# Dividing the attention numerators by their sum before the transposes, not after the weighted sum, from batch 1 on

## The chip, the cores and the metric

The kernel runs on one core of one Trainium2 chip. The metric is the time on the device in microseconds (us), the median of three runs. The core has five engines with a queue of their own each, and they meet only through semaphores: TensorE (PE in the profile, its weight loads PEld), VectorE (DVE), ScalarE (ACT), GpSimd (POOL) and SyncE (SP, which issues the DMAs). Every engine takes its queue in order.

## The reference, cut to what matters

The program is a top-32 attention over 8 batches, 8 heads, 576 positions and a head width of 64, and behind it a gated feed-forward network (FFN) over the 4608 tokens.

```python
scores = scale * np.matmul(q, k.transpose(0, 1, 3, 2))        # 8, 8, 576, 576
kth = np.partition(scores, -top_k, axis=-1)[..., -top_k:-top_k + 1]
scores = np.where(scores >= kth, scores, -1000000000.0)
scores = scores - np.max(scores, axis=-1, keepdims=True)
attn = np.exp(scores)
attn = attn / (np.sum(attn, axis=-1, keepdims=True) + 1e-09)
x = np.matmul(attn, v)                                        # tokens x 512, heads side by side
gate = 1.0 / (1.0 + np.exp(-(x @ w_gate)))
return gate * (x @ w_val) @ w_out
```

## The kernel before

**Steps.** Attention is cut into steps of one batch b, one row tile i and one pair of heads p. Tiles i = 0 to 3 hold 128 rows of two heads (J = 2 halves, called j = 0 and j = 1 below); tile i = 4 holds the last 64 rows of both heads in one half (J = 1). That makes 5 x 4 = 20 steps in a batch and 160 in all. A batch is walked in two groups of row tiles: 0 to 2 and 3 to 4 in an even batch, 0 to 1 and 2 to 4 in an odd one; within a group the four pairs follow each other.

**What a step does.** `scores` multiplies queries and keys on PE (L195) and ACT brings each half from PSUM into the tile `s` (L202). `select` finds the 32nd largest score of each row on DVE (L260 to L266, L286), helped by ACT (L272) and POOL (L278, L279), and ACT takes the exponentials into the tile `e` (L209). `masked` then sets what is below the threshold to zero and sums each row, in one DVE instruction for each half (L214); POOL adds 1e-9 to the sums in the small tile `st` (L217) and DVE takes the reciprocals (L218). POOL spreads the reciprocals over a 128 x 128 tile `inv` (L220), 64 columns for each head.

**Turning and weighing.** `turn` transposes `e` on PE in groups of three 128 x 128 blocks (L297, L302, L305); ACT copies each group from PSUM into `et` (L298, L303, L306). The first group needs half j = 0 alone, the second both halves, the third half j = 1. `weigh` multiplies `et` with the values on PE (L316 to L318 for full tiles, L321 to L324 for the last 64 rows), for one or two row tiles at once, into the left part `po` of one PSUM tile. Into the right part PE transposes `inv` of each of these row tiles (L327). ACT copies these spread reciprocals to SBUF as `rs` (L330), DVE multiplies `po` with them into `xf` (L333, L337), ACT rounds `xf` to the leading part `xh` (L340) and POOL subtracts to get the rest `xl` (L341). `xh` and `xl` are the FFN's input. `weigh` is called 112 times: 48 times with two row tiles (256 columns), 32 times with one (128 columns), and 32 times with the last 64 rows. So `inv` is turned 160 times.

**FFN.** Units of 384 tokens run as a generator beside the attention (`ffn`): 12 hidden blocks of 24 matmuls each (L372 to L374), gated by ACT, DVE and POOL (L377 to L380), and three rounds of output matmuls (L391 to L393). The loop in `run` takes pieces from the generators by the attention's progress, less a lag of 480 tokens (`BEHIND`). In the first 60 % of batch 0 the FFN's weights are split and stored too (`split_weight`, L116 to L148).

**What sets the order.** The program is written step by step with three stages in flight (`select` of step n, `masked` of step n-1, `turn` and `weigh` of step n-2), and the tile framework's scheduler then lays out each engine's queue from the dependences, its pools and its own estimates. Pools that matter here: `e` has three buffers, `et` two, the PSUM tile of `weigh` one, the PSUM of the scores one, of the transposes two, and of the FFN three. A second version of the whole program stands behind a test at the end (`run(True)`), for inputs on which the fast selection fails; it isn't executed here.

Of the kernel before, what the change touches and what calls it, by code (L numbers as in the profile page):

```python
# [15 lines left out]
AF = mybir.ActivationFunctionType  # L16
ALU = mybir.AluOpType
AX = mybir.AxisListType

TOPK = 32  # L20
# [8 lines left out]
def tile_topk_attention_then_gated_ffn(  # L29
# [8 lines left out]
    nc = tc.nc  # L38
# [3 lines left out]
    HALF = S // 2  # L42
# [19 lines left out]
    BEHIND = 480  # L62

    LOADED, HELD = 12, 0

    const = ctx.enter_context(tc.tile_pool(name="const", bufs=1))
    bi = ctx.enter_context(tc.tile_pool(name="bi", bufs=4))
# [25 lines left out]
    kths = const.tile([P, n_tiles + 8], F32, tag="kths", name="kths")  # L93
# [114 lines left out]
        for j in range(J):  # L208
            nc.scalar.activation(e[:, j], s[:, j], AF.Exp, bias=st[:, j : j + 1], scale=1.0 / SHRINK)  # L209

    def masked(J, s, kth, st, e, nm):

        for j in range(J):
            nc.vector.scalar_tensor_tensor(  # L214
                e[:, j], s[:, j], kth[j], e[:, j], op0=ALU.is_ge, op1=ALU.mult, accum_out=st[:, 4 + j : 5 + j]
            )
        nc.gpsimd.tensor_scalar(st[:, 4 : 4 + J], st[:, 4 : 4 + J], 1e-9, None, op0=ALU.add)  # L217
        nc.vector.reciprocal(st[:, 6 : 6 + J], st[:, 4 : 4 + J])  # L218
        inv = bi.tile([P, P], F32, tag="inv", name=f"inv_{nm}")
        nc.gpsimd.tensor_copy(  # L220
            inv.rearrange("p (j d) -> p j d", j=J), st[:, 6 : 6 + J].unsqueeze(2).to_broadcast([P, J, P // J])
        )
        return e, inv

    def select_any(J, s, nm):

        rest = b2.tile([P, 2, S + 8], F32, tag="u", name=f"rest_{nm}")[:, :, :S]
        tops = b2.tile([P, 2, TOPK], F32, tag="tops", name=f"tops_{nm}")
        st = bi.tile([P, 8], F32, tag="st", name=f"st_{nm}")
        e = b3.tile([P, 2, S], F32, tag="e", name=f"e_{nm}")  # L230
        for r in range(TOPK // 8):
            for j in range(J):
                t = tops[:, j, 8 * r : 8 * r + 8]
                src = rest[:, j] if r else s[:, j]
                nc.vector.max(t, src)
                if r < TOPK // 8 - 1:
                    nc.vector.match_replace(rest[:, j], t, src, LOWEST)
        nc.gpsimd.tensor_scalar(st[:, 0:J], tops[:, :J, 0], -1.0 / SHRINK, None, op0=ALU.mult)
        numerators(J, s, st, e)
        yield  # L240
        yield masked(J, s, [tops[:, j, TOPK - 1 :] for j in range(J)], st, e, nm)

    def select(J, s, col, nm):

# [37 lines left out]
        at = [n_tiles - col - j for j in range(J)]  # L284
        for j in range(J):
            nc.vector.max(kths[:, at[j] : at[j] + 8], u[:, j])  # L286
        yield masked(J, s, [kths[:, a + 7 : a + 8] for a in at], st, e, nm)

    def turn(e, i, et, o, nm):

# [17 lines left out]
    def weigh(et, vt, n, invs, pieces, nm):  # L308

        both = ps_o.tile([P, 4 * P], F32, tag="o", name=f"po_{nm}")  # L310
        po, rb = both[:, :n], both[:, 2 * P :]
        if n > REM:
            mixed = vt[:, 4:6].rearrange("p a d -> p (a d)")

            for c in reversed(range(4)):
                nc.tensor.matmul(po[D:], vt[:, 6 + c], et[:, 5 + c, :n], start=c == 3, stop=False)  # L316
                nc.tensor.matmul(po[:D], vt[:, c], et[:, c, :n], start=c == 3, stop=False)
            nc.tensor.matmul(po, mixed, et[:, 4, :n], start=False, stop=True)  # L318
        else:
            for c in range(4):  # L320
                nc.tensor.matmul(po[:D], vt[:, c], et[:, c, :REM], start=c == 0, stop=False)  # L321
                nc.tensor.matmul(po[D:], vt[:, 6 + c], et[:, c, REM:P], start=c == 0, stop=False)
            nc.tensor.matmul(po[:D], vt[:REM, 4], et[:REM, 4, :REM], start=False, stop=True)
            nc.tensor.matmul(po[D:], vt[:REM, 10], et[:REM, 4, REM:P], start=False, stop=True)  # L324

        for t, inv in enumerate(invs):
            nc.tensor.transpose(rb[:, t * P : (t + 1) * P], inv, ident)  # L327
        rs = b2.tile([P, 2 * P], F32, tag="rs", name=f"rs_{nm}")
        m = len(invs) * P
        nc.scalar.activation(rs[:, :m], rb[:, :m], AF.Copy)  # L330
        xf = b2.tile([P, 2 * P], F32, tag="xf", name=f"xf_{nm}")[:, :n]
        if n > REM:
            nc.vector.tensor_tensor(xf, po, rs[:, :n], op=ALU.mult)  # L333
        else:
            for h in range(2):
                d = slice(h * D, h * D + D)
                nc.vector.tensor_tensor(xf[d], po[d], rs[d, h * REM : h * REM + REM], op=ALU.mult)  # L337
        o = 0
        for (xh, xl), c, k in pieces:
            nc.scalar.activation(xh[:, c : c + k], xf[:, o : o + k], AF.Copy)  # L340
            nc.gpsimd.tensor_tensor(xl[:, c : c + k], xf[:, o : o + k], xh[:, c : c + k], op=ALU.subtract)  # L341
            o += k
# [61 lines left out]
    def run(general):  # L404
# [30 lines left out]
        parts, done = {}, {}  # L435

        for n in range(len(steps) + 2):
            if n < len(steps):
# [12 lines left out]
                J = 2 if i < NT else 1  # L451
                nm = f"{mark}{b}_{i}_{p}"
                if general:
                    parts[n] = select_any(J, staged.pop(n), nm)
                else:
                    parts[n] = select(J, staged.pop(n), col, nm)
                next(parts[n])
                col += J
            if n - 1 in parts:
# [113 lines left out]
```

## Time and profile before

| | before |
|---|---|
| median of 3 runs | 1626.93 us (1625.65 to 1627.8) |
| the profiled execution | 1628.2 us on the device, span 1626.3 us |
| PE busy | 1546.3 us, 95 % of the span |
| PE weight loads busy | 1399.8 us, 86 % |
| DVE busy | 1285.6 us, 79 % |
| POOL busy | 1238.9 us, 76 % |
| ACT busy | 1174.1 us, 72 % |
| mean granted TensorE clock | 0.977 of full speed |

The span runs from the first to the last instruction on the engines; the time on the device is 1.9 us more. Matmuls are pipelined: the profile gives each its whole passage through the array, so the durations of neighbours overlap, and the distance between their starts is shorter than the duration of one. Busy time is the union of what overlaps.

### The profile page before, as it was taken

The numbers are of one execution on the slowest core, as the hardware profiler recorded it, in microseconds if no ns is written. First come the engines' busy times: TensorE is split into PE (matmuls) and PEld (weight loads), VectorE is DVE, ScalarE is ACT, GpSimd is POOL, SyncE is SP. The second block draws the span as 40 slices with busy tenths as digits, with TensorE's granted clock in tenths as the row PEclk, the third lists the DMA queues.
The fourth block names the chain that finished last, engine by engine and source line by source line (L and its number), as shares of the span: only waits on it lengthen the run. The fifth ranks groups of instructions, "written<-read, shape, count | busy, mean of one in ns | idle before, by whom it ended". The sixth has DMA issues, their size and how long they took to land.

```text
span 1626.3 us, 33530 instructions
## 1 busy us (share of the span) xinstructions
PE 1546.3 (95%) x10226; PEld 1399.8 (86%) x10226; DVE 1285.6 (79%) x5748; ACT 1174.1 (72%) x2643; POOL 1238.9 (76%) x1959
## 2 busy tenths in 40 slices
PE   5777899899999999999999999999999999999998
PEld 3444797689999999989999999999899999999997
DVE  6999868988988778878888778889888778878310
ACT  8898668877777777677777777778677777767321
POOL 8889868898876887787776896788876987776413
PEclk8887999999999999999999999999999999999999
DMA  7546754566565665566564665565555665554574
GB/s 259 186 161 201 266 203 167 186 225 217 189 218 178 219 236 198 184 207 227 193 206 178 219 239 195 196 230 195 203 199 178 216 224 198 184 198 164 195 265 178
DMA packets 89182, 332.58 MB, mean 204 GB/s; under 512 B 9888, under 2 KB 36512, under 8 KB 62112
## 3 DMA queue, kind: packets, MB, share of 16 engines
q1 hardware_dynamic: 88992, 330.34, 58.7%
q8 instruction: 83, 1.36, 0.3%
q14 instruction: 107, 0.88, 0.2%
HBM read 301.99 MB, written 28.31 MB: 203 GB/s over the span
## 4 chain that ended last, share of the span: by engine, by line
PE 75%; DVE 5%; POOL 5%; ACT 4%; issue 1%; POOLq 0%; ACTq 0%; DVEq 0%
PE pz L372 11%; PE pz L374 11%; PE pz L373 11%; PE pss L195 8%; PE po L316 6%; PE pt L297 6%; PE po L391 6%; PE po L392 5%; PE po L393 5%; PE po L318 2%; POOL u L278 2%; DVE e L214 2%; ACT e L209 1%; PE po L327 1%; DVE kths L286 1%
## 5 line engine op out<-in xcount | busy, mean ns | idle before, releaser
L278 POOL TENSOR_TENSOR u<-s,under 128x288 f32<-128x288 f32 x576 | 446.1, 796 | 89.0 <-ACT under L272 82.7
L260 DVE MAX8 cand<-s 128x8 f32<-128x72 f32 x2304 | 346.7, 217 | 81.4 <-ACT s L202 80.7
L372 PE MATMUL pz<-xh,w 128*128 128x384 f32 x1120 | 383.3, 344 | 1.7 <-ACT part L398 1.7
L373 PE MATMUL pz<-xl,w 128*128 128x384 f32 x1120 | 379.5, 339 | 0.0
L374 PE MATMUL pz<-xh,w 128*128 128x384 f32 x1120 | 379.4, 339 | 0.0
L214 DVE SCALAR_TENSOR_TENSOR e<-s,kths,e 128x576 f32<-128x576 f32 x288 | 297.1, 1035 | 1.9 <-ACT e L209 1.8
L286 DVE MAX8 kths<-u 128x8 f32<-128x584 f32 x288 | 219.7, 763 | 71.0 <-POOL u L279 69.0
L272 ACT ACTIVATE under<-s,leads 128x576 bf16<-128x576 f32 x288 | 223.2, 776 | 42.2 <-DVE leads L264 38.0
L209 ACT ACTIVATE e<-s,st 128x576 f32<-128x576 f32 x288 | 210.7, 773 | 57.5 <-POOL st L268 57.4
L380 POOL TENSOR_TENSOR gl<-gf,gh 128x384 fp32r<-128x384 f32 x144 | 153.5, 1066 | 88.8 <-ACT gh L379 86.3
L202 ACT ACTIVATE s<-pss 128x576 f32<-128x576 f32 x288 | 185.3, 643 | 39.0 <-PE pss L195 38.9
L372 PEld LDWEIGHTS pz<-xh,w 128*128 128x128 f32 x1120 | 210.9, 188 | 2.5 <-ACT part L398 2.0
L195 PE MATMUL pss<-k,qh 128*128 128x288 f32 (+2 forms) x672 | 200.6, 316 | 13.1 <-ACT qh L176 6.6
L373 PEld LDWEIGHTS pz<-xl,w 128*128 128x128 f32 x1120 | 210.9, 188 | 0.4 <-issue 0.3
L374 PEld LDWEIGHTS pz<-xh,w 128*128 128x128 f32 x1120 | 210.7, 188 | 0.0
L298 ACT ACTIVATE et<-pt 128x384 f32<-128x384 f32 x384 | 180.8, 489 | 36.5 <-PE pt L297 35.6
L297 PE MATMUL pt<-ident,e 128*128 128x128 f32 x1152 | 188.0, 280 | 16.6 <-DVE e L214 14.9
L392 PE MATMUL po<-gl,w 128*128 128x384 f32 x560 | 192.2, 344 | 0.4 <-POOL gl L380 0.4
L391 PE MATMUL po<-gh,w 128*128 128x384 f32 x560 | 189.4, 352 | 1.8 <-ACT part L398 0.9
L393 PE MATMUL po<-gh,w 128*128 128x384 f32 x560 | 189.7, 340 | 0.0
L195 PE MATMUL pss<-k,ql 128*128 128x288 f32 (+2 forms) x672 | 185.1, 298 | 1.0 <-POOL ql L177 1.0
L297 PEld LDWEIGHTS pt<-ident,e 128*128 128x128 f32 x1152 | 145.4, 144 | 37.9 <-DVE e L214 16.2
(100 smaller groups left out, 3339.2 us busy)
## 6 DMA issues: line engine op xcount, KB each, us to landing
w<-ws SPq DMA_DIRECT2D x210, 1024.0 KB, 5.0
v<-in_v_dram SPq DMA_DIRECT2D x64, 352.0 KB, 3.4
qraw<-in_q_dram SPq DMA_DIRECT2D x160, 128.0 KB, 2.8
kraw<-in_k_dram SPq DMA_DIRECT2D x64, 288.0 KB, 3.4
wraw<-in_w_dram SPq DMA_DIRECT2D x36, 512.0 KB, 4.1
ws<-wsplit SPq DMA_DIRECT2D x36, 512.0 KB, 4.0
out_dram<-acc SPq DMA_DIRECT2D x48, 192.0 KB, 3.6
```

Source lines behind the costliest of these rows:

```text
L195: nc.tensor.matmul(ps[:, half, o : o + n], x[:, h * P : (h + 1) * P], ks[h][:, k0 : k0 + n], start=t == 0, stop=t == len(todo) - 1,)
L214: nc.vector.scalar_tensor_tensor(e[:, j], s[:, j], kth[j], e[:, j], op0=ALU.is_ge, op1=ALU.mult, accum_out=st[:, 4 + j : 5 + j])
L260: nc.vector.max(cand[:, j, 8 * g : 8 * g + 8], s[:, j, g * SEG : (g + 1) * SEG])
L278: nc.gpsimd.tensor_tensor(u[:, j, c], s[:, j, c], under[:, j, c], op=ALU.mult)
L286: nc.vector.max(kths[:, at[j] : at[j] + 8], u[:, j])
L297: nc.tensor.transpose(pt[:, c], ef[:, k0 : k0 + P], ident)
L372: nc.tensor.matmul(ps, wt[:, u, 0, d], xh, start=d == 0, stop=False)
L373: nc.tensor.matmul(ps, wt[:, u, 0, d], xl, start=False, stop=False)
L374: nc.tensor.matmul(ps, wt[:, u, 1, d], xh, start=False, stop=d == NP - 1)
L391: nc.tensor.matmul(ps, wt[:, e % 2, 0, f], gh, start=f == 0, stop=False)
L392: nc.tensor.matmul(ps, wt[:, e % 2, 0, f], gl, start=False, stop=False)
L393: nc.tensor.matmul(ps, wt[:, e % 2, 1, f], gh, start=False, stop=f == FG - 1)
```

## The change

From batch 1 on (`b < TURNED` with `TURNED = 1` keeps the old way for batch 0), the masked numerators `e` themselves are multiplied by the reciprocal of their row's sum, in place: half j = 0 in one instruction on ACT, half j = 1 (where there is one) in two instructions of 288 columns on POOL. No `inv` is made, none is transposed, and there are no `rs` and no `xf`: ACT rounds `po` straight from PSUM to `xh`, and DVE, which can read PSUM, subtracts to get `xl`.

```diff
-    def masked(J, s, kth, st, e, nm):
+    def masked(J, s, kth, st, e, turned, nm):
...
         nc.vector.reciprocal(st[:, 6 : 6 + J], st[:, 4 : 4 + J])
+        if not turned:
+            for j in range(J):
+                if j == 0:
+                    nc.scalar.activation(e[:, j], e[:, j], AF.Copy, scale=st[:, 6 + j : 7 + j])
+                    continue
+                for half in range(2):
+                    c = slice(half * HALF, (half + 1) * HALF)
+                    nc.gpsimd.tensor_scalar(e[:, j, c], e[:, j, c], st[:, 6 + j : 7 + j], None, op0=ALU.mult)
+            return e, None
         inv = bi.tile([P, P], F32, tag="inv", name=f"inv_{nm}")
...
+        o = 0
+        if invs[0] is None:
+            for (xh, xl), c, k in pieces:
+                nc.scalar.activation(xh[:, c : c + k], po[:, o : o + k], AF.Copy)
+                nc.vector.tensor_tensor(xl[:, c : c + k], po[:, o : o + k], xh[:, c : c + k], op=ALU.subtract)
+                o += k
+            return
         for t, inv in enumerate(invs):
             nc.tensor.transpose(rb[:, t * P : (t + 1) * P], inv, ident)
...
-                    parts[n] = select(J, staged.pop(n), col, nm)
+                    parts[n] = select(J, staged.pop(n), col, b < TURNED, nm)
```

The scheduler lays the queues out anew. Three places show how, all around batch 4, row tiles 0 to 2, pair 1. In the names the numbers behind a tile's name are batch, row tile and pair (then a buffer number); `gh`, `gl`, `po2`, `acc` and `w_5_...` belong to FFN unit 5. Line numbers are those of each kernel's own file.

PE's queue at the end of the weighing of row tiles 0 and 1, before:

```order
L317 MATMUL po_4_1_1_12522<-et_4_0_1_12349,v_8_1_11658 64x256
L318 MATMUL po_4_1_1_12522<-et_4_0_1_12349,v_8_1_11658 128x256
L327 MATMUL po_4_1_1_12522<-ident_102,inv_4_0_1_12138 128x128
L327 MATMUL po_4_1_1_12522<-ident_102,inv_4_1_1_12312 128x128
L297 MATMUL pt_4_2_1_1_12662<-ident_102,e_4_2_1_12267 128x128 x3
L297 MATMUL pt_4_2_1_2_12667<-ident_102,e_4_2_1_12267 128x128 x3
```

and in the changed kernel:

```order
L328 MATMUL po_4_1_1_12321<-et_4_0_1_12147,v_8_1_11468 64x256
L329 MATMUL po_4_1_1_12321<-et_4_0_1_12147,v_8_1_11468 128x256
L408 MATMUL po2_5_0_3_12567<-gh_5_0_0_11980,w_5_13_12549 128x384
L409 MATMUL po2_5_0_3_12567<-gl_5_0_0_11981,w_5_13_12549 128x384
L410 MATMUL po2_5_0_3_12567<-gh_5_0_0_11980,w_5_13_12549 128x384
```

The two transposes of `inv` are gone, and FFN matmuls follow the last product directly; the transposes of row tile 2, which stood behind them, come later.

POOL's queue around the reciprocals of row tile 1, before:

```order
L177 TENSOR_TENSOR ql_4_0_3_12247<-qraw_4_0_3_12244,qh_4_0_3_12246 128x256
L217 TENSOR_SCALAR st_4_1_1_12091<-st_4_1_1_12091 128x2
L220 COPY inv_4_1_1_12312<-st_4_1_1_12091 128x128
L268 TENSOR_SCALAR st_4_2_1_12265<-tops_4_2_1_12264 128x2
L380 TENSOR_TENSOR gl_5_0_1_12317<-gf_5_0_1_12344,gh_5_0_1_12316 128x384
```

and in the changed kernel:

```order
L397 TENSOR_TENSOR gl_5_0_2_12237<-gf_5_0_2_12264,gh_5_0_2_12236 128x384
L219 TENSOR_SCALAR st_4_1_1_11892<-st_4_1_1_11892 128x2
L228 TENSOR_SCALAR e_4_1_1_11894<-e_4_1_1_11894,st_4_1_1_11892 128x288 x2
L179 TENSOR_TENSOR ql_4_1_3_12166<-qraw_4_1_3_12163,qh_4_1_3_12165 128x256
L289 TENSOR_TENSOR u_4_2_1_12065<-s_4_2_1_11727,under_4_2_1_12066 128x288 x2
```

Where the copy to `inv` stood, directly behind the addition of 1e-9, the two multiplications of half j = 1 stand now; between the two on POOL lies the reciprocal on DVE, as before.

ACT's queue in the changed kernel, from the exponentials of row tile 2 to the first copy of the transposed row tile 1:

```order
L211 ACTIVATE e_4_2_1_12064<-s_4_2_1_11727,st_4_2_1_12062 128x576 x2
L394 ACTIVATE gf_5_0_3_12299<-pz_5_0_3_0_12273 128x384
L224 ACTIVATE e_4_1_1_11894<-e_4_1_1_11894,st_4_1_1_11892 128x576
L178 ACTIVATE qh_4_1_3_12165<-qraw_4_1_3_12163 128x256
L204 ACTIVATE s_4_0_2_11877<-pss_4_0_2_1_11884 128x576
L283 ACTIVATE under_4_2_1_12066,sums_4_2_1_12063<-s_4_2_1_11727,leads_119 128x576
L396 ACTIVATE gh_5_0_3_12271<-gf_5_0_3_12299 128x384
L283 ACTIVATE under_4_0_2_12188,sums_4_0_2_12185<-s_4_0_2_11877,leads_119 128x576
L309 ACTIVATE et_4_0_1_12147<-pt_4_1_1_0_12304 128x3x128
```

The division of half j = 0 (L224) is a new row in this queue. It stands six rows ahead of the copy of the first transposed blocks of the same tile, with an eviction of scores (L204), two rows of the selection (L283) and two of other work between.

## Rows read from the trace of the kernel before

**Rows 1.** Busy time of each engine in four stretches of the span, in us: while batch 0 ends, in the middle, while the attention runs out, and (the last row) from 200 to 1500 us as a whole. The columns are the stretch, its length, and the busy us (and instructions) of PE, PEld, DVE, ACT and POOL, then the granted clock, the DMAs' share and GB/s.

```profile
150.00:200.00 50.00, 39.79 (x258) 33.17 (x257) 45.16 (x166) 34.75 (x78) 46.83 (x71) 0.93 0.71 251
...
700.00:900.00 200.00, 200.00 (x1375) 186.86 (x1375) 169.70 (x777) 146.89 (x334) 154.08 (x250) 1.00 0.60 205
...
1500.00:1560.00 60.00, 60.00 (x398) 56.52 (x397) 18.75 (x60) 21.98 (x50) 24.75 (x35) 1.00 0.59 206
...
200.00:1500.00 1300.00, 1284.89 (x8804) 1188.97 (x8804) 1080.51 (x4948) 972.24 (x2217) 1021.28 (x1641) 1.00 0.59 203
```

**Rows 2.** The page's chain of work that ended last, as shares of the span by engine and by engine and line.

```profile
PE 75%; DVE 5%; POOL 5%; ACT 4%; issue 1%; POOLq 0%; ACTq 0%; DVEq 0%
PE pz L372 11%; PE pz L374 11%; PE pz L373 11%; PE pss L195 8%; PE po L316 6%; PE pt L297 6%; PE po L391 6%; PE po L392 5%; PE po L393 5%; PE po L318 2%; POOL u L278 2%; DVE e L214 2%; ACT e L209 1%; PE po L327 1%; DVE kths L286 1%
```

**Rows 3.** Pieces of the same chain in order of time, around two calls of `weigh` near 805 and 812 us: start, us on the chain, what. A pair of transposes of `inv` ends the first call, a single one the second.

```profile
804.69 0.63 PE po L318 x2
805.32 0.22 PE po L327 x2
...
812.47 0.20 PE po L323
812.73 0.26 PE po L327
812.99 0.33 PE pt L297 x3
```

**Rows 4.** Groups of instructions by line over the whole span, shapes of one line put together: line, engine, operation, tiles and first shape, count | busy us, mean ns of one | idle time of the engine before them, and what ended it.

```profile
L327 PE MATMUL po<-ident,inv 128*128 128x128 f32 x160 | 38.0, 286 | 0.0
...
L209 ACT ACTIVATE e<-s,st 128x576 f32<-128x576 f32 x288 | 210.7, 773 | 57.5 <-POOL st L268 57.4
...
L330 ACT ACTIVATE rs<-po 128x256 f32<-128x256 f32 (+1 forms) x112 | 35.7, 319 | 51.9 <-PE po L327 51.8
...
L340 ACT ACTIVATE xh<-xf 128x64 fp32r<-128x64 f32 (+3 forms) x128 | 39.8, 323 | 28.7 <-DVE xf L337 15.7 <-DVE xf L333 12.7
...
L220 POOL COPY inv<-st 128x128 f32<-128x128 f32 x160 | 54.0, 338 | 37.6 <-DVE st L218 34.2 <-DVE tops L264 0.7 <-DVE bad L511 0.3
...
L341 POOL TENSOR_TENSOR xl<-xf,xh 128x64 fp32r<-128x64 f32 (+3 forms) x128 | 73.5, 579 | 21.1 <-ACT xh L340 18.9
...
L333 DVE TENSOR_TENSOR xf<-po,rs 128x256 f32<-128x256 f32 (+1 forms) x80 | 28.7, 358 | 11.6 <-ACT rs L330 11.1
...
L337 DVE TENSOR_TENSOR xf<-po,rs 64x64 f32<-64x64 f32 x64 | 13.8, 215 | 8.0 <-ACT rs L330 7.4
```

**Rows 5.** Groups of POOL from 200 to 1500 us, in the same columns with the shapes kept apart: the copy to `inv`, the smallest multiplication by a constant, and the product of scores and mask with its two tensors of 288 columns.

```profile
L220 POOL COPY inv<-st 128x128 f32<-128x128 f32 x139 | 45.5, 328 | 34.6 <-DVE st L218 31.7 <-DVE tops L264 0.7
...
L217 POOL TENSOR_SCALAR st<-st 128x2 f32<-128x2 f32 x111 | 26.5, 239 | 42.9 <-DVE e L214 36.9
...
L278 POOL TENSOR_TENSOR u<-s,under 128x288 f32<-128x288 f32 x503 | 382.0, 781 | 82.8 <-ACT under L272 77.6 <-PE pt L297 0.7 <-PE pz L374 0.6
```

**Rows 6.** Who waited for whom: engine and line, for what, us in total, times, longest. The first two are PE's from 200 to 1500 us, the third is PE's from 0 to 200 us, the fourth POOL's from 200 to 1500 us.

```profile
PE pss L195 <- ACT s L202: 3.1, 4, 1.1
...
PE pt L297 <- DVE e L214: 0.5, 1, 0.5
...
PE pt L297 <- DVE e L214: 14.4, 14, 2.7
...
POOL inv L220 <- DVE st L218: 31.7, 56, 1.6
```

**Rows 7.** Single instructions in order of time (start us, us, engine, line): POOL and DVE while step b 4, i 0, p 1 is masked, and the transposes of that step on PE. Its three groups of blocks start at 815.10 (the other two blocks follow at 815.92), 817.91 and 820.15 us.

```profile
807.41 1.15 DVE L214 SCALAR_TENSOR_TENSOR e<-s,kths,e 128x576 f32<-128x576 f32 x1
...
809.01 0.80 DVE L214 SCALAR_TENSOR_TENSOR e<-s,kths,e 128x576 f32<-128x576 f32 x1
...
810.54 0.15 DVE L218 RECIPROCAL st<-st 128x2 f32<-128x2 f32 x1
...
806.51 1.43 POOL L278 TENSOR_TENSOR u<-s,under 128x288 f32<-128x288 f32 x2
808.02 0.60 POOL L268 TENSOR_SCALAR st<-tops 128x2 f32<-128x2 f32 x1
809.91 0.22 POOL L217 TENSOR_SCALAR st<-st 128x2 f32<-128x2 f32 x1 [1.28 <-DVE e L214]
...
815.10 0.27 PE L297 MATMUL pt<-ident,e 128*128 128x128 f32 x1
...
817.91 0.49 PE L297 MATMUL pt<-ident,e 128*128 128x128 f32 x3
...
820.15 0.49 PE L297 MATMUL pt<-ident,e 128*128 128x128 f32 x3
```

More of the change, by code (lines that the diff above doesn't have):

```diff
@@ L64, in tile_topk_attention_then_gated_ffn @@
     LOADED, HELD = 12, 0
+    TURNED = 1
     const = ctx.enter_context(tc.tile_pool(name="const", bufs=1))
@@ L223, in masked, with select_any @@
         return e, inv
-    def select_any(J, s, nm):
+    def select_any(J, s, turned, nm):
         rest = b2.tile([P, 2, S + 8], F32, tag="u", name=f"rest_{nm}")[:, :, :S]
@@ L240, in select_any, with select @@
         yield
-        yield masked(J, s, [tops[:, j, TOPK - 1 :] for j in range(J)], st, e, nm)
-    def select(J, s, col, nm):
+        yield masked(J, s, [tops[:, j, TOPK - 1 :] for j in range(J)], st, e, turned, nm)
+    def select(J, s, col, turned, nm):
         cand = b2.tile([P, 2, NSEG * 8], F32, tag="cand", name=f"cand_{nm}")
@@ L286, in select @@
             nc.vector.max(kths[:, at[j] : at[j] + 8], u[:, j])
-        yield masked(J, s, [kths[:, a + 7 : a + 8] for a in at], st, e, nm)
+        yield masked(J, s, [kths[:, a + 7 : a + 8] for a in at], st, e, turned, nm)
     def turn(e, i, et, o, nm):
@@ L337, in weigh @@
                 nc.vector.tensor_tensor(xf[d], po[d], rs[d, h * REM : h * REM + REM], op=ALU.mult)
-        o = 0
         for (xh, xl), c, k in pieces:
@@ L453, in run @@
                 if general:
-                    parts[n] = select_any(J, staged.pop(n), nm)
+                    parts[n] = select_any(J, staged.pop(n), b < TURNED, nm)
                 else:
-                    parts[n] = select(J, staged.pop(n), col, nm)
+                    parts[n] = select(J, staged.pop(n), col, b < TURNED, nm)
                 next(parts[n])
```

## The prediction, written before the changed kernel ran

> **What bounds the kernel now.** I read the busy time by stretch first. From 200 to 1500 us PE is busy 1284.9 of 1300 us at the full granted clock, while DVE has 1080.5, POOL 1021.3 and ACT 972.2 us [rows 1]. Between 700 and 900 us PE has no idle time that the profile shows. Before 200 us it is otherwise: as batch 0 ends, PE is busy 39.8 of 50 us and POOL 46.8 [rows 1]. The chain of waits says the same from the other end: 75 % of the span lies on PE, 5 % each on DVE and POOL, 4 % on ACT [rows 2]. PE's own waits show how little it is held up behind 200 us: the largest is 3.1 us for evictions of scores, and for masked numerators it waited once, 0.5 us [rows 6].
>
> So from 200 us on time is PE's work. The FFN's matmuls are the reason: the scheduler fills with them whatever the selection leaves open. What shortens PE's queue shortens the span, as long as PE doesn't begin to wait; what is added elsewhere costs nothing, as long as that engine keeps up.
>
> **PE: what is removed.** Of 160 steps 20 belong to batch 0, so 140 transposes of `inv` go. What one is worth is read from the chain, where neighbours don't overlap: a pair takes 0.22 us, so 0.11 each, and a single one behind the last 64 rows takes 0.26 [rows 3]. By the loops, the seven batches have 44 calls with a pair and 24 with one full row tile, 112 transposes, and 28 calls with the last 64 rows. That is 112 x 0.11 = 12.3 us and 28 x 0.11 to 0.26 = 3.1 to 7.3 us, since part of the 0.26 is the passage from narrow products, which whatever follows may have to pay too. In sum 15.4 to 19.6; I take 17. The outer bounds are further away. PE's busy time has 38.0 / 160 = 0.24 us for one [rows 4], so 33 us if each were worth that; and nothing if the time freed turns into waits. The page's chain gives this line 1 % of the span, some 16 us for all 160 [rows 2], which sides with the lower price.
>
> **ACT.** Added are 140 divisions of 128 x 576. The nearest row is the exponential of the same shape in SBUF, 0.773 us [rows 4], so 108 us. Removed is `rs`, 35.7 us x 7/8 = 31 us [rows 4]. The roundings to `xh` now read PSUM; `rs` did so at 0.319 us on average and `xh` took 0.323 from SBUF over a similar mix of sizes [rows 4], so nothing there. Net +77 us, against 328 us in which ACT is idle between 200 and 1500 us [rows 1]. It would be busy some 82 %, and hides it if the new row doesn't stand in front of something that PE needs. The division waits for a reciprocal, a wait that ACT didn't have; queued behind it are an eviction of scores, parts of the selection and the copies of transposed blocks. The same wait on POOL, for `inv`, cost 31.7 us in 139 steps, 0.23 us each [rows 6]. On ACT I expect between nothing and that, and none of it on PE.
>
> **POOL.** Removed are 140 copies at 0.338 us, 47 us, and `xl`, 73.5 x 7/8 = 64 us [rows 4]. Added are 112 x 2 = 224 multiplications of 128 x 288 by one number per row. The trace has none of that size. From below: the copy of 128 columns takes 0.328 us and the multiplication of 2 columns 0.239, so 0.71 ns a column and 0.239 + 286 x 0.00071 = 0.44 us [rows 5]. From above: the product of two tensors of 288 columns, 0.781 us [rows 5]. With one tensor to read it is nearer to the copy; I take 0.44, so 99 us and a balance of -13 us. At 0.78 it is 175 us and a balance of +63 us, which 279 us of idle time [rows 1] would still hold.
>
> The Trainium skill (GPSIMD Engine Reference, Engine selection) says that GpSimd is about twice as slow as VectorE on two inputs and roughly at line rate on one; no row here has a single input of that size. By it a column costs one cycle of a 1.2 GHz engine, 0.24 us for 288, and with the 0.24 us of the smallest multiplication the price would be 0.48 us, an estimate; the sum would stay the same.
>
> **DVE.** Removed are the products with `rs`, (28.7 + 13.8) x 7/8 = 37 us; added are 112 subtractions that read `po` too. By the rows of those products each takes 0.215 to 0.358 us [rows 4], so 24 to 40 us. Balance -13 to +3 us on an engine with 220 us of idle time [rows 1]. They wait for `xh` on ACT as the products waited for `rs` (11.1 + 7.4 us in all [rows 4]); what queues behind, the next selection, queued behind that before. DVE and POOL also slow each other: the masking took 1.15 us while POOL worked and 0.80 us while it sat idle [rows 7]. POOL's busy time changes by -1 to +6 % of its 1021 us, so this hardly moves.
>
> **The path from masking to transposes.** This is what grows. In the step of rows 7 masking ends at 809.8 us, the reciprocal at 810.7, and the first block, of half 0, is turned at 815.1; the second group, the first to need half 1, at 817.9. The division adds 0.77 us on ACT to half 0 and 2 x 0.44 on POOL to half 1. The cushion behind the reciprocal is 4.4 and 7.2 us here, enough for the work and a queue of several instructions. Cover for PE, if a step comes later, is the FFN work in its queue, as long as the scheduler put it there: in the new order FFN products do stand behind the weighing, and the turning comes later than it did. I cost this at nothing; without that cover it is the second rival.
>
> **The sum.** PE -17 us, the rest hidden. The profiled execution took 1628.2 us, 1.9 more than its span of 1626.3, and stands 1.3 above the median of 1626.9. 1628.2 - 17 = 1611.2 for an execution like it, so 1610 for the median.
>
> **Rivals.**
>
> *The time comes back as waits elsewhere, no change.* The selection's chain (scores, selection, mask, exponentials, masking) could set the pace, and PE's idle time would only be hidden by the long durations the profile gives matmuls. For it: DVE is at 83 %, and the chain does leave PE for POOL, DVE and ACT, 14 % of the span in all [rows 2]. Against it: while the attention runs out, from 1500 to 1560 us, PE is busy throughout with DVE at a third [rows 1], so there is FFN work left that PE could have done earlier had it had time. 1627 us, 12 %.
>
> The Trainium skill (Perfetto Trace Analysis, Identifying the Most-Contended Engine) says that matmul busy time is a bad measure of TensorE's headroom and that the weight loads' busy share is a good one. Here the weight loads are busy 1189 of 1300 us, 91 % [rows 1], which by that rule leaves more room than the matmul row shows and speaks for this rival; by its rule the sum could be nothing.
>
> *PE waits for divided numerators, slower.* The queues are laid out by estimates, and ACT's or POOL's new rows may come later than planned, at the first transposes of a step. In the first 200 us, where PE's cover is thin, it waited 14 times for masked numerators, 14.4 us, so 1.03 us each [rows 6]. If one step of four did so from batch 1 on, 35 x 1.03 = 36 us: 1610 + 36 = 1646 us. It decides from 17 / 1.03 = 17 such waits in 140 steps. For it: two engines more on the path. Against it: the cushion of rows 7, and the single wait of 0.5 us behind 200 us. 14 %.
>
> *More than the chain's price.* If each transpose is worth its busy time of 0.24 us, 140 x 0.24 = 33 us go: 1594 us. For it: the single one at 0.26 [rows 3]. Against it: the pairs. 10 %.
>
> **How the numbers follow.** Forecast 64 %, 1610 us, its own range 1604 to 1618 (15 to 20 us removed and a few of waits or of a new layout in batch 0's overlap). The range that should hold 8 in 10 takes in no change and the mild end of the slower rival, and part of the larger gain: 1597 to 1632. A measurement of this kernel tells 0.2 %, 3.3 us, from no change. Faster: 64 + 10 = 74 %; within it 12 %; slower 14 %.
>
> **What would show it.** Right: 20 transposes of `inv` left, PE still busy about 99 % from 200 us to the end of the attention, the attention's last step and the span both some 17 us earlier, POOL's multiplications near 0.44 us and its busy time about as before, ACT's up by some 77 us. Wrong: a line of PE waiting at its transposes for ACT's or POOL's products, or for evictions of scores, of more than 10 us in all; POOL's multiplications near 0.8 us with late `gl` behind them; or a PE that is less busy than before in the middle with the same span.

## The result, and the profile after

The changed kernel took 1641.88 us, the median of 4 runs (1641.09 to 1642.79), beside 1627.05 us for the kernel before on the same chip: a ratio of 1.0091, with a 95 % interval of 1.0075 to 1.0107. It is slower by 15 us. The forecast was 1610 us in a range of 1597 to 1632: the sign is wrong, and the time lies outside the range.

The top of the page of the profiled execution, whose span is 1640.4 us:

```profile
PE 1538.7 (94%) x10086; PEld 1386.6 (85%) x10086; DVE 1270.6 (77%) x5736; ACT 1236.5 (75%) x2687; POOL 1373.7 (84%) x1931
```

The work moved as the diff says. PE has 140 instructions fewer (10086, and 20 transposes of `inv` are left), ACT 62 us more (I had 77; its rows by themselves sum to some 75, and in the busy time neighbours overlap). POOL, which was to lose 13 us, has 135 us more (1238.9 before). The groups by line, in the columns of [rows 4], and below them the one line's spread (ns, least, median, most):

```profile
L228 POOL TENSOR_SCALAR e<-e,st 128x288 f32<-128x288 f32 x224 | 235.5, 1060 | 30.4 <-DVE st L220 27.8 <-PE pt L308 0.4 <-PE pz L391 0.4
...
L224 ACT ACTIVATE e<-e,st 128x576 f32<-128x576 f32 x140 | 108.6, 775 | 34.5 <-DVE st L220 34.2
...
L341 DVE TENSOR_TENSOR xl<-po,xh 128x256 fp32r<-128x256 f32 (+2 forms) x112 | 33.0, 294 | 21.0 <-ACT xh L340 20.5
```

```profile
L228 POOL TENSOR_SCALAR e<-e,st x224: 997/1009/1638, 238.8 to 1526.5; 128x288 f32<-128x288 f32 x112
```

ACT's division costs what was taken for it (0.775 us against 0.773), and so does the subtraction on DVE (0.294, between 0.215 and 0.358). POOL's multiplication took 1.06 us on average where I took 0.44 and set 0.781 as the upper bound [rows 5]. Even the quickest of the 224 took 0.997, and the nine during which DVE stood idle for over nine tenths of the time took 1.00 to 1.01. So DVE's work beside it isn't the cause of the price: it is the instruction.

Busy time by stretch, in the columns of [rows 1]:

```profile
150.00:200.00 50.00, 39.72 (x256) 32.70 (x254) 44.91 (x166) 34.50 (x78) 46.82 (x72) 0.93 0.71 251
200.00:1500.00 1300.00, 1263.35 (x8560) 1162.88 (x8559) 1055.61 (x4888) 1023.60 (x2238) 1146.18 (x1601) 0.99 0.58 201
700.00:900.00 200.00, 195.94 (x1316) 180.97 (x1316) 163.51 (x767) 157.48 (x343) 174.24 (x248) 0.99 0.58 201
```

Until 200 us the two kernels are alike. From there to 1500 us POOL is busy 1146 us, 88 %, and PE, busy 1284.9 of 1300 us before, now 1263.4. The idle time goes from 15 to 37 us. It is spread over the whole stretch: between 700 and 900 us PE now has 4 us of it, and before had none. PE's waits from 200 to 1500 us (for what, us in total, times, longest):

```profile
PE pss L197 <- ACT s L204: 7.0, 8, 2.2
PE pt L308 <- POOL e L228: 3.9, 4, 2.1
PE po L409 <- POOL gl L397: 3.2, 3, 1.3
PE pz L389 <- ACT xh L340: 3.1, 3, 1.4
...
PE pt L308 <- ACT e L224: 1.8, 2, 1.4
```

No wait stands out. PE waits for the divided numerators 6 times, 5.7 us in all, and otherwise for a bit of everything. After such a wait the clock can be lower too. The longest of them, 2.12 us, ends at 747.99 us, and from there to 751.3 us the granted clock was the lower of TensorE's two levels, 1.2 instead of 2.4 GHz: the FFN's products start 0.32 us apart, where they started 0.17 apart before the wait (start us, us, instruction, idle time before it; then the stretch in the columns of [rows 1]).

```profile
743.00 0.33 PE L408 MATMUL po<-gh,w 128*128 128x384 f32 x1
743.17 0.33 PE L409 MATMUL po<-gl,w 128*128 128x384 f32 x1
...
747.99 0.69 PE L308 MATMUL pt<-ident,e 128*128 128x128 f32 x2 [2.12 <-POOL e L228]
...
749.44 0.52 PE L408 MATMUL po<-gh,w 128*128 128x384 f32 x1
749.76 0.52 PE L409 MATMUL po<-gl,w 128*128 128x384 f32 x1
```

```profile
747.90:751.30 3.40, 3.31 (x11) 3.31 (x12) 2.87 (x18) 0.49 (x1) 3.24 (x6) 0.51 0.90 315
```

From 200 to 1500 us the trace has 13.7 us at that level in four places; the kernel before has 10.2.

The chain, in the columns of [rows 2], has moved off PE all the same, from 75 % to 50 %, and POOL, DVE and the time between instructions took it up:

```profile
PE 50%; POOL 12%; DVE 11%; ACT 5%; issue 3%; DMA 1%; POOLq 0%; ACTq 0%; SPq 0%; DVEq 0%
```

What such a stretch looks like, as pieces of the chain in order of time (start us, us on the chain, what):

```profile
679.62 2.63 POOL e L228 x2
682.25 1.39 POOL u L289 x2
683.65 0.09 issue
683.74 0.23 POOL st L219
683.99 0.17 DVE st L220
```

The two multiplications occupy POOL for 2.63 us. Behind them in POOL's queue stand the product that starts the next selection (`u`, L289) and the addition of 1e-9 to the next step's sums (L219). The masking of the next step, on DVE, had by then ended (start us, us, instruction; the second row stores the sum of the second half):

```profile
679.57 0.81 DVE L216 SCALAR_TENSOR_TENSOR e<-s,kths,e 128x576 f32<-128x576 f32 x1
680.30 0.08 DVE L216 DVE_READ_ACCUMULATOR e<-s,kths,e 128x1 f32 x1
...
683.99 0.17 DVE L220 RECIPROCAL st<-st 128x2 f32<-128x2 f32 x1 [1.24 <-POOL st L219]
```

The sums were there at 680.4 us, and the addition began at 683.74. DVE had other rows to do for most of that time, so the reciprocal came 1.24 us late, and the division of half 0 on ACT 0.73 us:

```profile
684.19 0.78 ACT L224 ACTIVATE e<-e,st 128x576 f32<-128x576 f32 x1 [0.73 <-DVE st L220]
```

A long instruction that nobody needs soon delays short ones that somebody needs now.

### The profile page after: what moved, and what is told of

The parts are those of the page before. It is cut to its first block, busy times and chain, and to the rows that moved or that the text cites. A ratio compares the mean times of both kernels' runs of the same rounds, so it can differ in the third digit from the quotient of the medians.

```text
span 1640.4 us, 33374 instructions
## 1 busy us (share of the span) xinstructions
PE 1538.7 (94%) x10086; PEld 1386.6 (85%) x10086; DVE 1270.6 (77%) x5736; ACT 1236.5 (75%) x2687; POOL 1373.7 (84%) x1931
## 4 chain that ended last, share of the span: by engine, by line
PE 50%; POOL 12%; DVE 11%; ACT 5%; issue 3%; DMA 1%; POOLq 0%; ACTq 0%; SPq 0%; DVEq 0%
PE pz L389 8%; PE pz L390 8%; PE pz L391 8%; PE pss L197 5%; PE pt L308 4%; POOL u L289 4%; PE po L408 4%; PE po L409 4%; PE po L410 4%; PE po L327 4%; DVE e L216 3%; DVE cand L271 3%; DVE kths L297 2%; POOL e L228 2%; POOL k L165 2%
## 5 line engine op out<-in xcount | busy, mean ns | idle before, releaser
L289 POOL TENSOR_TENSOR u<-s,under 128x288 f32<-128x288 f32 x576 | 453.9, 810 | 37.6 <-ACT under L283 30.6
L228 POOL TENSOR_SCALAR e<-e,st 128x288 f32<-128x288 f32 x224 | 235.5, 1060 | 30.4 <-DVE st L220 27.8
L283 ACT ACTIVATE under<-s,leads 128x576 bf16<-128x576 f32 x288 | 223.5, 777 | 46.7 <-DVE leads L275 38.3
L397 POOL TENSOR_TENSOR gl<-gf,gh 128x384 fp32r<-128x384 f32 x144 | 157.1, 1092 | 84.3 <-ACT gh L396 81.1
L204 ACT ACTIVATE s<-pss 128x576 f32<-128x576 f32 x288 | 186.4, 647 | 40.8 <-PE pss L197 40.3
L410 PE MATMUL po<-gh,w 128*128 128x384 f32 x560 | 188.6, 339 | 0.0
L408 PE MATMUL po<-gh,w 128*128 128x384 f32 x560 | 184.7, 347 | 4.2 <-ACT part L415 1.8
```

Source lines behind the costliest of these rows:

```text
L228: nc.gpsimd.tensor_scalar(e[:, j, c], e[:, j, c], st[:, 6 + j : 7 + j], None, op0=ALU.mult)
L289: nc.gpsimd.tensor_tensor(u[:, j, c], s[:, j, c], under[:, j, c], op=ALU.mult)
L410: nc.tensor.matmul(ps, wt[:, e % 2, 1, f], gh, start=False, stop=f == FG - 1)
```

## Experiments 1: is it GpSimd's time?

Three accounts were set against each other: that POOL's added time delays its other work; that the divisions lie on the path from masking to transposes; and that the new order of the queues itself is worse. Where a kernel below leaves divisions out, its diff shows which, and its time is that of the work left.

**e1, both halves on ACT.**

```diff
-                if j == 0:
-                    nc.scalar.activation(e[:, j], e[:, j], AF.Copy, scale=st[:, 6 + j : 7 + j])
-                    continue
-                for half in range(2):
-                    c = slice(half * HALF, (half + 1) * HALF)
-                    nc.gpsimd.tensor_scalar(e[:, j, c], e[:, j, c], st[:, 6 + j : 7 + j], None, op0=ALU.mult)
+                nc.scalar.activation(e[:, j], e[:, j], AF.Copy, scale=st[:, 6 + j : 7 + j])
```

> Both halves are divided on ACT; POOL has no multiplication. Theory LOAD (POOL's 224 multiplications of about 1.06 us load its queue, and everything that passes through POOL comes late to PE): POOL's busy time falls from 1374 to about 1140 us and the time to about 1612 us, the 17 us forecast from PE's removed transposes. Theory PATH (any division between masking and transposes makes PE wait for numerators): both halves now wait on one engine, so 1640 us or more. Theory LAYOUT (any new order of the queues costs some 15 us): about 1640 us.

Measured: 1678.97 us, ratio 1.0324 [1.0307, 1.0341]. POOL is down to 1126.5 us busy, and the kernel is another 37 us slower. The first row of PE's waits from 200 to 1500 us says where:

```profile
PE pss L197 <- ACT s L204: 27.7, 25, 3.0
PE pt L303 <- ACT e L223: 5.3, 6, 1.8
```

ACT's evictions of scores are late; for divided numerators PE waits 5.3 us, no more than in the changed kernel. LOAD missed, and the time is where PATH put it, but not by the wait that PATH names. This is a new cost, on another engine, so the miss says nothing against POOL's part in the changed kernel.

**e2, the kernel before with POOL's load alone:** 224 multiplications of a tile that nobody reads, two behind each masking of a step with two halves, from batch 1 on.

```diff
+        if loaded and J == 2:
+            for half in range(2):
+                nc.gpsimd.tensor_scalar(junk, junk, ident[:, 0:1], None, op0=ALU.mult)
```

> The kernel before, with 224 multiplications of 128 x 288 of a tile that nothing else uses added to POOL from batch 1 on; nothing is added between masking and transposes, and no transpose is removed. LOAD: POOL's busy time goes to about 1475 us, more than in the changed kernel, so 1650 us or more. PATH: no change, 1627 us. LAYOUT: about 1640 us.

Measured: 1667.0 us, 1.0251 [1.0234, 1.0268]; POOL busy 1472.8 us. Load on POOL alone, which no instruction waits for, costs 40 us. But the scheduler also laid the queues out anew around it.

**e3, no division from batch 1 on:** the loop over j is left out, all else of the change stays.

> The changed kernel without the division in batches 1 to 7 (left out: neither ACT nor POOL multiplies, so the output there isn't divided by the sums). It shows what the removed transposes, copies and products are worth by themselves. LOAD and PATH: 1605 to 1612 us. LAYOUT: about 1640 us.

Measured: 1622.09 us, 0.9973 [0.9964, 0.9983]. Without any added work the change gains less than 5 us of the 17 I had put down: between what LOAD and PATH expected and what LAYOUT did, so none of the three held.

**e4, the multiplications as products of two tensors.**

```diff
-                    nc.gpsimd.tensor_scalar(e[:, j, c], e[:, j, c], st[:, 6 + j : 7 + j], None, op0=ALU.mult)
+                    nc.gpsimd.tensor_tensor(e[:, j, c], e[:, j, c], st[:, 6 + j : 7 + j].to_broadcast([P, HALF]), op=ALU.mult)
```

> POOL multiplies half 1 by the reciprocals as a second tensor that is read again and again, in place of one number per row. By the row of the two-tensor product one takes 0.78 us in place of 1.06, so POOL gives back some 60 us of 1374. LOAD: about half of the way back, 1622 to 1634 us. PATH and LAYOUT: about 1640 us.

```profile
L228 POOL TENSOR_TENSOR e<-e,st 128x288 f32<-128x288 f32 x224 | 155.0, 712 | 42.7 <-DVE st L220 38.7 <-PE pt L310 1.1 <-DVE tops L277 0.9
```

Measured: 1647.11 us, 1.013 [1.0113, 1.0147]. The same product costs 0.712 instead of 1.06 us, POOL has 78 us less to do, and the kernel is slower by 5 us than the changed one. By POOL's time alone it had to be faster. PE waited 16.0 us for evictions of scores here, against 7.0. Something other than POOL's time changes between these builds.

## Experiments 2: how much is the order?

**e7, POOL's half alone, and e8, ACT's half alone:** in e7 the activation for j = 0 is left out, in e8 the two multiplications for j = 1.

> The changed kernel with the division of half 0 on ACT left out (half 0 of batches 1 to 7 isn't divided); POOL still multiplies half 1. Without any division the time was 1622, with both 1642. If POOL's queue is what costs: about 1640. If ACT's queue is: about 1623. If the two add: in between, 1630.

> The changed kernel with the multiplications of half 1 on POOL left out (half 1 of batches 1 to 7 isn't divided); ACT still divides half 0. If ACT's queue is what costs: about 1640. If POOL's queue is: about 1623. If the two add: the rest of the 20 us that the other run leaves.

Measured: e7 1633.33 us, 1.0039 [1.0025, 1.0054]; e8 1664.76 us, 1.0221 [1.0197, 1.0246]. Beside e3 that is +11 for POOL's half and +43 for ACT's, while both together make +20. These don't add up: e8 does strictly less than the changed kernel and takes 23 us more.

**e9, the kernel before with another lag.** `BEHIND` decides how far the FFN's pieces stand behind the attention; no instruction is added or removed.

```diff
-    BEHIND = 480
+    BEHIND = 440
```

> The kernel before with the FFN's lag set to 440 tokens in place of 480: the same instructions in another order. Theory LAYOUT (the old order is a lucky one among orders that lie some 10 us apart): 1632 to 1645 us. LOAD (time goes by the engines' loads): 1627 within 3 us.

> The kernel before with a lag of 520 tokens. LAYOUT: 1632 to 1645 us, LOAD: 1627 within 3 us, as with 440.

Measured: 1642.95 us at 440 (1.0096 [1.0078, 1.0114]) and 1635.62 at 520 (1.0055 [1.0036, 1.0075]). The same instructions in another order take 9 to 16 us more. The lag isn't a neutral redraw of the order, though: it also decides how much of the FFN is left when the attention is over. The attention's last product at 440, 480 and 520 (ns, then first and last start us):

```profile
L324 PE MATMUL po<-et,v x64: 217/243/268, 176.5 to 1560.9; 64*64 64x64 f32 x64
L324 PE MATMUL po<-et,v x64: 218/266/367, 176.1 to 1537.0; 64*64 64x64 f32 x64
L324 PE MATMUL po<-et,v x64: 218/267/367, 176.9 to 1532.3; 64*64 64x64 f32 x64
```

The spans are 1642.5, 1626.3 and 1632.6 us, so 81.6, 89.3 and 100.3 us lie behind it. At 520 the attention ends 5 us earlier than at 480, and the end of the FFN takes 11 us longer. So 480 may suit this kernel, and not be a lucky draw; how far orders scatter at one lag was not tested by itself. That orders do differ at one lag is seen in e8, which does less than the changed kernel and takes 23 us more. So kernels whose queues differ can't be compared for less than such amounts, and none of e1 to e8 can price an instruction by itself.

**e10, the changed kernel at 520.**

> The changed kernel with the FFN's lag at 520 tokens, another order of the same instructions. With the kernel before, 440 and 520 were 16 and 9 us slower than 480. If orders of the changed kernel scatter as much, anything from 1627 to 1658; LENGTH as the main cause: not below 1630 us.

Measured: 1635.37 us, 1.0048 [1.0031, 1.0064]. Both accounts allowed this time. At this lag the kernel before (1635.62) and the changed one take the same time, by another division of it: the attention's last product starts at 1540.2 us in the changed kernel and at 1532.3 before, and 92.7 and 100.3 us lie behind it. The 15 us are those of one pair of orders, and the order before the change was the best of its three.

## Experiments 3: the same queues, only shorter instructions

To price the instructions, the queues must stay. In the next five kernels the program is laid out in full, and only then are the chosen instructions cut to their first 8 columns: same instructions, same order, same semaphores.

```python
small = [copy.replace(a, ap=[parts, [1, columns]], bass_ap=None) for a in (o, x)]   # columns = 8
block.instructions[at] = copy.replace(i, outs=[small[0], *i.outs[1:]], ins=[small[1], *i.ins[1:]])
```

**s1, POOL's multiplications short; s2, ACT's divisions short; s3, both** (in the changed kernel's queues; beyond 8 columns the numerators stay undivided).

> The queues of the changed kernel, instruction for instruction; but after they were laid out, each of POOL's multiplications was cut from 288 columns to 8 (the other columns of half 1 aren't divided). POOL loses some 180 us of work and nothing else changes place. Theory LENGTH (the time that the new rows occupy POOL and ACT is the cause): 1620 to 1630 us. Theory ORDER (the order in which the queues were laid out, with the waits for the reciprocals, is the cause): 1637 to 1642 us.

> The same queues, with ACT's divisions cut from 576 columns to 8 (the other columns of half 0 aren't divided); POOL as in the changed kernel. ACT loses some 75 us of work. LENGTH: 1630 to 1637 us, since ACT has more idle time than POOL. ORDER: 1637 to 1642 us.

> The same queues, with both cut to 8 columns (nearly all of batches 1 to 7 isn't divided). LENGTH: 1610 to 1622 us, as low as or lower than the kernel without division at 1622. ORDER: 1630 us or more.

Measured: s1 1619.31 us, 0.9949 [0.9933, 0.9966]; s2 1641.89, 1.0085 [1.0068, 1.0102]; s3 1617.76, 0.994 [0.9924, 0.9957]. Against the 1641.88 of the changed kernel, the length of POOL's multiplications is worth 22.6 us and that of ACT's divisions nothing. (With POOL's already short, s1 against s3, ACT's are worth 1.5 us.) LENGTH held for POOL (s1 lies just under its 1620) and missed for ACT. The group and the stretch of s1:

```profile
L228 POOL TENSOR_SCALAR e<-e,st 128x8 f32<-128x8 f32 x224 | 81.3, 373 | 34.4 <-DVE st L220 30.9 <-PE pt L308 0.9 <-PE pz L391 0.5
```

```profile
200.00:1500.00 1300.00, 1276.72 (x8724) 1180.14 (x8722) 1063.65 (x4975) 1041.82 (x2276) 1006.15 (x1630) 1.00 0.59 203
```

The multiplications fell from 1060 to 373 ns, 154 us of POOL's time in all, and PE gets 164 more instructions done in the same 1300 us; at 1300 / 8724 = 0.149 us each that is 24 us. Of it 13.4 us show as less idle time of PE. Up to 5 more are the clock: of these 1300 us PE worked 13.6 at 1.2 GHz in the changed kernel and 2.9 in s1, and half of the difference is what the lower level can have cost. The rest, some 6 us, isn't seen in either; it may lie in PE's busy row, since the profile gives each matmul its whole passage and shows no idle time where one starts late within that of the one before.

How POOL's time may reach PE is seen in who waits for POOL's short rows, from 200 to 1500 us. The changed kernel:

```profile
DVE kths L297 <- POOL u L290: 56.3, 51, 3.0
ACT e L211 <- POOL st L279: 38.0, 40, 2.9
...
DVE st L220 <- POOL st L219: 29.9, 40, 2.3
```

and s1, with the same queues:

```profile
DVE kths L297 <- POOL u L290: 29.3, 22, 3.2
...
DVE st L220 <- POOL st L219: 11.9, 22, 1.1
...
ACT e L211 <- POOL st L279: 9.9, 11, 2.5
```

Three handovers inside a step go through POOL: the product for the selection, the offset that the exponentials need, and the sums. Waits for them fall from 124 to 51 us in these queues. Between queues their sum tells nothing: the kernel before has 138 us of them and takes 1627 us,

```profile
DVE kths L286 <- POOL u L279: 66.0, 66, 3.2
ACT e L209 <- POOL st L268: 52.5, 43, 3.5
...
DVE st L218 <- POOL st L217: 19.3, 28, 1.5
```

and e3, with 182, takes 1622. So these are the rows that POOL's long ones delay; which of the delays PE's FFN work doesn't cover, and how they reach PE, isn't shown.

**s6, e2's queues with its dead multiplications cut to 8 columns.**

> The queues of the kernel before with 224 multiplications added to POOL (1667 us), with those cut to 8 columns. LENGTH: back to 1627 to 1635 us. ORDER: 1655 us or more.

Measured: 1633.26 us, 1.0035 [1.0023, 1.0048], beside 1667.0 of e2. Their length is worth 33.7 us, for 161 us of POOL's time (247.2 to 86.2 us busy), where nothing waits for their result. So it is the queue behind them: no numerators pass through these rows. (Waits for the three handovers fall too, from 99 to 14 us.) In the changed kernel s1 shortens the queue and the path of half 1 at once; PE's 3.9 us of waits for POOL's products there are all that shows of the path. POOL's time also costs more per us here, 0.21 instead of 22.6 / 154 = 0.15, on a POOL that is fuller (94 % of 200 to 1500 us in e2):

```profile
200.00:1500.00 1300.00, 1265.21 (x8603) 1167.43 (x8602) 1058.12 (x4837) 952.84 (x2168) 1219.06 (x1821) 0.99 0.57 201
```

**s7, e8's queues with ACT's divisions cut.**

> The queues of the kernel that divides half 0 on ACT alone (1665 us, although POOL has 235 us less to do than in the changed kernel), with ACT's divisions cut to 8 columns (nothing is divided but those). LENGTH: near the kernel without division, 1620 to 1630 us. ORDER (this order of the queues is a bad one by itself): 1650 us or more.

Measured: 1649.98 us, 1.0135 [1.0118, 1.0152]. Of the 43 us by which e8 lies above e3, 15 are the length of ACT's divisions, and 28 are there without it: that is e8's order. In those queues PE waits 16.3 us for evictions of scores even with the short divisions, where e3 has 2.9. ORDER had it nearly right, LENGTH missed. From 200 to 1500 us PE idles 49.7 us in e8, 42.4 in s7 and 19.7 in e3, and it worked 36.6, 24.8 and 16.6 us at the lower clock, half of which can count as lost: beside e3 that makes 30 + 10 of e8's 43 us and 23 + 4 of s7's 28. So PE's idle time and the lower clock hold nearly all of it; which row of that order is at fault wasn't found.

## Experiments 4: another place for the divisions

**e5, POOL multiplies by the constant 0.1** in place of the row's reciprocal (two executions).

> The changed kernel with POOL multiplying half 1 by a constant in the instruction and not by a number per row read from SBUF (half 1 is not divided by its sums, and POOL doesn't wait for the reciprocal). It measures the price: if the number per row is what makes one multiplication take 1.06 us, 0.4 to 0.5 us; if it is the size, 1.0. LENGTH: 1622 to 1632 us at the low price.

```profile
L228 POOL TENSOR_SCALAR e<-e x224: 929/937/1490, 238.3 to 1535.6; 128x288 f32<-128x288 f32 x112
```

The median falls from 1009 to 937 ns. Reading the number from a tile is 0.07 us of the price; the other 0.94 are the multiplication of 288 columns with its fixed part. The low price that the expectation allowed for, 0.4 to 0.5 us, is out. The time, 1651.53 us (1.0146 [1.0126, 1.0166]), belongs to yet another order and prices nothing.

**e6, half 1 on DVE** (`nc.vector.tensor_scalar` over 576 columns), **and e13, both halves on DVE.**

> The changed kernel with half 1 divided on DVE in one instruction of 576 columns, half 0 still on ACT. POOL has no multiplication and is as free as in the shortened queues. LENGTH: between 1618 and 1632 us, by what DVE takes for it. ORDER (any order with ACT's division at its place is slow): 1640 us or more.

> Both halves are divided on VectorE (one instruction of 128 x 576 each), none on ScalarE and GpSimd. LENGTH (GpSimd's full queue is what costs): GpSimd and ScalarE have less to do than in any version that divides, VectorE gets about 252 x 0.4 us more on an engine with some 245 us of idle time from 200 to 1500 us: 1622 to 1632. VECTOR (VectorE, which carries the selection and the masking, is then the engine that is late): 1636 or more, with PE's waits for tiles of VectorE growing.

Measured: e6 1631.45 us, 1.0025 [1.0015, 1.0034]; e13 1638.43 us, 1.0071 [1.0055, 1.0088]. DVE does 576 columns in 0.652 us (e6), less than POOL does 288. e6 computes all the changed kernel does and is 10 us faster, though still 4 us behind the kernel before; as the queues differ, the 10 us can't be put down to POOL's row alone. In e13 LENGTH missed and the time is in VECTOR's range. One division took DVE 0.691 us there, not the 0.4 taken; with 85 % of the span on DVE, PE waits 5.8 us for DVE's products, and idles 35 us from 200 to 1500 us, nearly as much as in the changed kernel. The order may have its part in this too; the two weren't separated. Its two largest waits there:

```profile
PE pss L197 <- ACT s L204: 6.9, 8, 2.0
PE pt L303 <- DVE e L223: 5.8, 5, 3.0
```

**e15, e6 with a lag of 520.**

> The kernel with half 1 divided on VectorE (1631.45) in the order of a lag of 520 tokens. ORDER: the lag shifts a kernel by some 6 to 16 us in either direction whatever it divides, so anything from 1620 to 1645 is possible and the result won't keep the distance of 0 us that the changed kernel and the kernel before had at 520. ADDITIVE (the lag adds the same to each version): the kernel before went from 1627 to 1636, so this one goes to about 1640.

Measured: 1634.7 us, 1.005 [1.0033, 1.0067]. At 520 the three placements (1635.62, 1635.37, 1634.7) can't be told apart, at 480 they spread over 15 us. ADDITIVE missed, and of ORDER the part that the distance of 0 us would not last: it did. What the lag adds is no constant: +9, -7 and +3 us. No version that computes the whole output beat the kernel before.

## Why the prediction was wrong

**The step that failed: "With one tensor to read it is nearer to the copy; I take 0.44", and its bound "From above: the product of two tensors of 288 columns, 0.781 us".** The price measured is 1.06 us, above the bound. The row taken from below was a copy of a broadcast, and the multiplication of 2 columns holds little but the fixed part: neither shows what a column of the multiplication costs on POOL. It is some 2.4 ns by the rows of now, (1060 - 373) / 280 between the changed kernel and s1, and (937 - 239) / 286 with the constant, against the 0.71 that I carried over. And the bound wasn't one: e4 shows the two-tensor product of the same tile at 0.712, so one operand fewer was no reason for less. The balance on POOL is +135 us instead of -13.

The Trainium skill (GPSIMD Engine Reference, Engine selection) has GpSimd roughly at line rate on one input; the 0.48 us worked out from that isn't borne out by 1.06, nor by the 0.937 of e5, which reads no second operand, and the measurement decides.

s1 shows that this is the step. There the multiplications cost 0.373 us, near the price assumed, and the changed queues take 1619.3 us: faster than before by 0.5 %, within the range, 9 us above the forecast. This holds for the queues at a lag of 480; at 520 one multiplication took 1.05 us as well, and the changed kernel was level with the one before.

**The second step: "At 0.78 it is 175 us and a balance of +63 us, which 279 us of idle time [rows 1] would still hold", and before it "what is added elsewhere costs nothing, as long as that engine keeps up".** POOL did keep up by that measure: from 200 to 1500 us it was still idle for 154. But it takes its queue in order, and a step goes through it three times, so the length of a row in front can be handed on long before the engine is full: what s1 takes off POOL is worth 22.6 us of time, what s6 takes off 33.7. So even at 0.781 the load couldn't be put down at nothing: 224 x (0.781 - 0.373) = 91 us more than in s1 make some 13 us at s1's 0.15, an estimate, so 1633 us, and the range lacked its upper end.

**PE, -17 us: nearly right.** From the start of the last product of a full tile's call to the start of the second FFN product behind it I read 613 ns with two transposes of `inv` between and 390 without, 0.11 us each as [rows 3] had it; behind the last 64 rows it is 491 and 429, so 0.06. That is 112 x 0.11 + 28 x 0.06 = 14 us. In s3, where hardly any division is left, the kernel is 9.3 us faster. The 5 us between weren't traced to a cause; waits of the new order may be in them, and the short multiplications, whose 81 us on POOL take up most of the 111 us that left it. So: -14 us of PE's work, +5 of the rest, +24 for the length of both divisions (s3 to the changed kernel), +15 in sum. Where the end comes from is seen in the attention's last product, L335 (ns, then first and last start). In the changed kernel and in s1:

```profile
L335 PE MATMUL po<-et,v x64: 218/267/367, 176.2 to 1552.1; 64*64 64x64 f32 x64
```

```profile
L335 PE MATMUL po<-et,v x64: 218/242/267, 175.9 to 1529.2; 64*64 64x64 f32 x64
```

The 22.9 us between the last starts are the whole of what s1 is faster by: the FFN's tail only follows.

**ACT: right.** Its 140 divisions took 108.6 us, and by s2 they cost nothing in the time. But that holds for this order: in e8's they cost 15 us. (By the prediction's own terms ACT would have been busy 972 + 77 of 1300 us, 81 % and not 82; it was 79.) DVE's balance, put at -13 to +3 us, was -15.

**The path from masking to transposes: right as far as it went.** PE waited 5.7 us for divided numerators, 6 times, well short of the 36 us of the rival "PE waits for divided numerators". That rival's time, 1646 us, came close by another mechanism: s6 shows a loss of that kind with products that nobody reads.

**The rival of no change** said that the selection's chain could set the pace. It lost as written: s1 turns 7.7 of PE's saved 14 us into time. Its ground was sound, though: 14 % of the chain [rows 2] lay on POOL, DVE and ACT before, and this is the part that grew, to 28 %.

**What was not priced at all is the order.** Another lag moved the kernel before by +9 and +16 us without any change of instructions, as much as the whole expected gain, and e8's queues cost 28 us at the same lag. A forecast of -17 us with an own range of 1604 to 1618 left out that the new layout is a draw of its own. Open is what makes e4's and e8's orders bad ones, and whether the changed kernel has a lag at which it beats 1627 us: of its lags only 480 and 520 were run.

## What to carry to other kernels

Price an instruction by a row of the same operation and a like number of columns; a two-tensor product is no ceiling for a product with one number per row on GpSimd, and without such a row the upper end stays open. An engine that hands on small results in the middle of a chain can have less room than its idle time says: ask what stands in its queue behind the added row, and who waits for that. Where a scheduler lays out the queues anew, differences of about 1 % can come from the order alone, so to price one instruction cut its length in the finished queues and leave everything else.

## What the hardware showed that was not expected

On GpSimd the multiplication of a 128 x 288 tile of f32 by one number per row took 1.06 us on average, 1.009 in the median and 0.997 at least, by a constant 0.937 in the median, and as a product of two tensors, one of them a broadcast of the same number, 0.712 on average. VectorE took 0.652 us for 576 columns by one number per row (e6).
